# A fused attention and MoE kernel: a written-out order that interleaves one batch's attention with the preceding batch's MoE, heads in pairs on TensorE, attention output made transposed

## The chip, the core and the metric

One core of one Trainium2 chip runs the whole program. The metric is device time in microseconds (us), the median of several executions. The engines are named as in the profile: PE (TensorE; PEld are its weight loads), DVE (VectorE), ACT (ScalarE), POOL (GpSimd) and SP (SyncE, which here only issues transfers). Each works through its own queue in order; an instruction that waits holds up what is behind it on that engine.

## The reference

Two stages with sizes B = 8 batches, H = 12 heads, S = 448 positions, D = 64, and for the MoE 3584 tokens, 768 model columns and 2048 hidden columns; everything is float32 outside.

```python
def _attn_ref(q, k, v, g_q, g_k):
    def rmsnorm(x, g):
        rms = np.sqrt(np.mean(x * x, axis=-1, keepdims=True) + 1e-06)
        return x / rms * g
    q_n, k_n = (rmsnorm(q, g_q), rmsnorm(k, g_k))
    scores = np.matmul(q_n, k_n.transpose(0, 1, 3, 2)) / np.sqrt(q.shape[-1])
    ...
    return softmax(scores) @ v

def _moe_ref(x, w_in, w_out, alpha):      # x: heads side by side, one row per token
    h = x @ w_in
    s = np.sin(alpha * h)
    g = h + s * s / (alpha + 1e-09)
    return g @ w_out
```

The quotation writes the softmax in one line; "snake" below means the step from h to g.

## The kernel before

It is written with a tile framework whose scheduler orders the instructions of each engine by itself and places every wait. There are two stages, one after the other.

**Attention** (L70 to L151) runs over 8 batches and, in each, over 6 pairs of heads. q, k and v of a whole batch come by one transfer each (L80 to L82; 112 positions on the partitions, four blocks of them), v on POOL's queue because it is cast to bf16. Per head DVE squares and sums q and k (L92, L93), ACT takes the root (L95), DVE the reciprocal (L97) and, for each block of 112 positions, scales and multiplies by the gain (L99). PE transposes a pair's blocks (L109, L112), and DVE copies each from PSUM (L110, L113). Then, for each head, four score matmuls contract over that head's 64 partitions (L125), and ACT's Exp writes the weights with keys on the partitions (L129). The product with V (L133) holds a 112 by 112 piece of the weights stationary and streams V's 64 columns with a column of ones beside them (L120, L121): 16 matmuls of 65 columns per head, so that the output has positions on the partitions and the softmax sum in column 65. DVE divides (L140, L141), and because the MoE wants model columns on the partitions, PE transposes the result again (L147) and DVE copies it into `xT` (L148). All eight batches of `xT` stay in SBUF.

**MoE** (L160 to L213) holds both weight matrices in SBUF; their transfers (L169, L170) are issued on POOL's queue once the attention stage's SBUF is free. Over 8 groups of 448 tokens: for each of 16 blocks of 128 hidden columns, six matmuls (L183) make `hps`, ACT takes Sin (L190), DVE squares (L192) and adds (L193) into `g_sb`. Then, for each of four blocks of 112 tokens and two halves of 384 columns, 16 matmuls (L201), a copy (L208) and a store of 168 KB (L209).

Of the kernel before, what the change touches and what calls it, by code (L numbers as in the profile page):

```python
# [25 lines left out]
ALU = mybir.AluOpType  # L26


@with_exitstack
def kernel(  # L30
# [11 lines left out]
):  # L42
    nc = tc.nc
    B, H, S, D = q.shape
    N_TOK = B * S
    D_MODEL = H * D
    D_FF = moe_w_in.shape[1]
    KT = D_MODEL // 128
    MT = D_FF // 128
    P = 128  # L50

    SCORE_SCALE = float(D) ** 0.5

    SQB = 4
    SKB = 4
    sq_sz = S // SQB
    sk_sz = S // SKB

    const = ctx.enter_context(tc.tile_pool(name="const", bufs=1))
    gq_sb = const.tile([P, 1, D], F32)  # L60
# [4 lines left out]
    make_identity(nc, ident)  # L65

    xpool = ctx.enter_context(tc.tile_pool(name="xT", bufs=1))
    xT_b = [xpool.tile([P, KT, S], BF16, tag=f"xT{bb}", name=f"xT{bb}") for bb in range(B)]

    with tc.tile_pool(name="attn_in", bufs=2) as ain, \  # L70
         tc.tile_pool(name="attn_w", bufs=3) as awork, \
         tc.tile_pool(name="attn_wT", bufs=2) as awT, \
         tc.tile_pool(name="attn_sc", bufs=3, space=bass.MemoryType.PSUM) as scps, \
         tc.tile_pool(name="attn_tp", bufs=2, space=bass.MemoryType.PSUM) as tpps, \
         tc.tile_pool(name="attn_av", bufs=3, space=bass.MemoryType.PSUM) as avps:
        for b in range(B):
            qall = ain.tile([sq_sz, H, SQB, D], F32, tag="qall")
            kall = ain.tile([sq_sz, H, SQB, D], F32, tag="kall")
            vall = ain.tile([sq_sz, H, SQB, D], BF16, tag="vall")
            nc.sync.dma_start(out=qall, in_=q[b].rearrange("h (t p) d -> p h t d", p=sq_sz))  # L80
            nc.sync.dma_start(out=kall, in_=k[b].rearrange("h (t p) d -> p h t d", p=sq_sz))
            nc.gpsimd.dma_start(out=vall, in_=v[b].rearrange("h (t p) d -> p h t d", p=sq_sz))  # L82
            for hp in range(H // 2):
                h0 = 2 * hp
                qn = awork.tile([sq_sz, SQB, 2 * D], BF16, tag="qn")
                kn = awork.tile([sq_sz, SQB, 2 * D], BF16, tag="kn")
                for hi in range(2):
                    h = h0 + hi
                    for (xin, xout, gs) in ((qall[:, h], qn, gq_sb), (kall[:, h], kn, gk_sb)):
# [154 lines left out]
```

## Time and profile before

| what | value |
|---|---|
| median of three runs (lowest, highest) | 1063.31 us (1063.0, 1063.66) |
| span of the profiled execution | 1061.3 us |
| mean granted TensorE clock over the span | 0.995 |
| one transfer of q, k: size, median from issue to landing | 1344 KB, 8.6 us and 18.8 us |
| one transfer of v: size as stored, median from issue to landing | 672 KB, 15.1 us |
| bytes read from HBM, written | 45.69 MB, 11.01 MB |

The profile is of one execution. A busy time is the time in which an engine had at least one instruction running, so a group's busy time divided by its count can be less than its mean duration: matmuls overlap in PE's pipeline. "Idle before" is how long an engine stood still just ahead of a group's instructions, with an arrow to what ended that. The chain of waits goes back from the last instruction to what released each step. The granted clock is TensorE's, as a share of full speed. In tables of stretches times are counted from the span's start.

### The profile page before, as it was taken

How to read it: one execution, taken by the hardware profiler on the slowest of the kernel's cores; microseconds unless marked ns; L12 is line 12 of the kernel's file. 1: busy time of each engine (PE TensorE's matmuls, PEld its weight loads, DVE VectorE, ACT ScalarE, POOL GpSimd, SP SyncE). 2: the span in 40 equal slices, each digit the busy share in tenths (PEclk: the TensorE clock that was granted, in tenths of full speed). 3: DMA queues.
4: the chain of work that ended last, by engine and by line, in shares of the span. 5: the costliest groups of instructions: out<-in, count | busy, mean ns of one | idle time of the engine just before them, and what ended most of it. 6: DMA issues, size and time to landing. Idle time of an engine off the chain costs nothing.

```text
span 1061.3 us, 13360 instructions
## 1 busy us (share of the span) xinstructions
PE 813.0 (77%) x4288; PEld 486.0 (46%) x4288; DVE 697.4 (66%) x3201; ACT 422.4 (40%) x801; POOL 18.7 (2%) x16
## 2 busy tenths in 40 slices
PE   0677777777777777777777777737999999999998
PEld 0334444444444444444443444413656656656665
DVE  0777777777777777777777777613575665665754
ACT  0444445555445544555544554412131231221221
POOL 1000000000000000000000000000000000000000
PEclk9999999999999999999999999998999999999999
DMA  9701800900900900810540000075101101101001
GB/s 148 114 1 31 101 0 1 131 1 1 130 1 1 130 1 1 99 33 1 74 57 1 1 0 1 1 130 108 46 7 53 41 14 53 33 20 53 23 31 53
DMA packets 142870, 45.75 MB, mean 43 GB/s; under 512 B 132816, under 2 KB 142032, under 8 KB 142800
## 3 DMA queue, kind: packets, MB, share of 16 engines
q1 hardware_dynamic: 96816, 33.11, 15.9%
q0 software_dynamic: 45984, 11.80, 11.1%
q8 instruction: 33, 0.54, 0.2%
q14 instruction: 37, 0.30, 0.1%
HBM read 45.69 MB, written 11.01 MB: 53 GB/s over the span
## 4 chain that ended last, share of the span: by engine, by line
PE 60%; DVE 22%; ACT 9%; DMA 6%; issue 2%; SPq 0%; POOL 0%; ACTq 0%
PE av L133 17%; PE ops L201 16%; PE hps L183 13%; PE sc L125 12%; DVE kn L99 7%; ACT L129 6%; DVE qn L99 4%; DMA w_out_sb<-in_moe_w_out_dram 3%; DMA kall<-in_k_dram 2%; ACT expT L129 2%; DVE xT L148 2%; DVE invs L140 2%; DVE qT L110 2%; DVE ssq L93 2%; PE tp L109 1%
## 5 line engine op out<-in xcount | busy, mean ns | idle before, releaser
L133 PEld LDWEIGHTS <-expT 112*112 112x112 bf16 x1536 | 164.3, 204 | 147.6 <-DVE outn L141 56.7
L129 ACT ACTIVATE expT<-sc 112x448 bf16<-112x448 f32 x384 | 187.8, 544 | 73.2 <-PE sc L125 72.7
L133 PE MATMUL av<-vA,expT 112*112 112x65 bf16 x1536 | 202.2, 286 | 18.4 <-DVE outn L141 18.3
L125 PE MATMUL sc<-qT,kT 64*112 64x448 bf16 x384 | 193.6, 580 | 18.5 <-ACT expT L129 9.3
L183 PE MATMUL hps<-xT,w_in_sb 128*128 128x448 bf16 x768 | 169.4, 360 | 26.4 <-DMA w_in_sb<-in_moe_w_in_dram 17.5
L201 PE MATMUL ops<-w_out_sb,g_sb 128*112 128x384 bf16 x1024 | 185.6, 327 | 5.2 <-DMA w_out_sb<-in_moe_w_out_dram 5.2
L190 ACT ACTIVATE s<-hps,alpha_sb 128x448 f32<-128x448 f32 x128 | 81.1, 634 | 242.5 <-PE hps L183 207.9
L109 PE MATMUL tp<-ident,qn 112*128 112x112 bf16 x192 | 49.6, 258 | 140.1 <-DVE qn L99 101.8
L140 DVE RECIPROCAL invs<-av 112x1 f32<-112x1 f32 x384 | 50.3, 168 | 160.5 <-PE av L133 160.2
L201 PEld LDWEIGHTS <-g_sb 128*112 128x112 bf16 x1024 | 132.0, 130 | 49.5 <-issue 5.7
L95 ACT ACTIVATE rms<-ssq 112x4 f32<-112x4 f32 x192 | 29.1, 197 | 279.6 <-DVE ssq L93 273.2
L192 DVE TENSOR_TENSOR s<-s 128x448 f32<-128x448 f32 x128 | 79.8, 624 | 80.2 <-ACT s L190 80.2
L183 PEld LDWEIGHTS <-w_in_sb 128*128 128x128 bf16 x768 | 75.8, 99 | 101.6 <-issue 44.8
L193 DVE SCALAR_TENSOR_TENSOR g_sb<-s,inv_alpha_sb,hps 128x448 bf16<-128x448 f32 x128 | 87.0, 680 | 4.5
L208 DVE COPY osb<-ops 112x384 f32<-112x384 f32 x64 | 34.2, 555 | 74.7 <-PE ops L201 63.4
L99 DVE SCALAR_TENSOR_TENSOR qn<-qall,inv_rms,gq_sb 112x64 bf16<-112x64 f32 x384 | 83.3, 278 | 0.0
L99 DVE SCALAR_TENSOR_TENSOR kn<-kall,inv_rms,gk_sb 112x64 bf16<-112x64 f32 x384 | 83.0, 278 | 0.0
L125 PEld LDWEIGHTS <-kT 64*112 64x112 bf16 x384 | 64.3, 182 | 39.3 <-issue 25.6
L93 DVE TENSOR_REDUCE ssq<-sqv 112x4 f32<-112x256 f32 x192 | 74.5, 408 | 0.1
L109 PEld LDWEIGHTS <-qn 112*128 112x128 bf16 x192 | 20.6, 107 | 117.2 <-DVE qn L99 114.4
L112 PE MATMUL tp<-ident,kn 112*128 112x112 bf16 x192 | 49.3, 257 | 25.3 <-DVE kn L99 24.6
L141 DVE TENSOR_TENSOR outn<-av,invs 112x64 bf16<-112x64 f32 x384 | 65.5, 212 | 0.2
(24 smaller groups left out, 481.3 us busy)
## 6 DMA issues: line engine op xcount, KB each, us to landing
qall<-in_q_dram SPq DMA_DIRECT2D x8, 1344.0 KB, 8.6
kall<-in_k_dram SPq DMA_DIRECT2D x8, 1344.0 KB, 18.8
out_dram<-osb SPq DMA_DIRECT2D x64, 168.0 KB, 2.1
vall<-in_v_dram POOLq DMA_DIRECT2D x8, 672.0 KB, 15.1
w_in_sb<-in_moe_w_in_dram POOLq DMA_DIRECT2D x1, 3072.0 KB, 17.9
w_out_sb<-in_moe_w_out_dram POOLq DMA_DIRECT2D x1, 3072.0 KB, 32.7
gq_sb<-in_g_q_dram SPq DMA_DIRECT2D x1, 32.0 KB, 3.2
gk_sb<-in_g_k_dram SPq DMA_DIRECT2D x1, 32.0 KB, 4.4
```

The source lines that it names most:

```text
L93: nc.vector.reduce_sum(ssq, sqv, axis=AX.X)
L99: nc.vector.scalar_tensor_tensor(xout[:, t, hi * D:(hi + 1) * D], xin[:, t, :], inv_rms[:, t:t + 1], gs[:sq_sz, 0, :], op0=ALU.mult, op1=A ...
L109: nc.tensor.transpose(tp, qn[:, t, :], ident[:sq_sz, :sq_sz])
L125: nc.tensor.matmul(sc[:, :S], kT[pbase:pbase + D, t * sk_sz:(t + 1) * sk_sz], qT[pbase:pbase + D, :], start=True, stop=True,)
L129: nc.scalar.activation(expT[:, t, :], sc[:, :S], ACT.Exp, scale=SCORE_SCALE)
L133: nc.tensor.matmul(av, expT[:, t, u * sq_sz:(u + 1) * sq_sz], vA[:, t, :], start=(t == 0), stop=(t == SKB - 1),)
L140: nc.vector.reciprocal(invs, av[:, D:D + 1])
L183: nc.tensor.matmul(hps, w_in_sb[:, kt, m * P:(m + 1) * P], xT[:, kt, :], start=(kt == 0), stop=(kt == KT - 1),)
L190: nc.scalar.activation(s1, hps, ACT.Sin, scale=alpha_sb[:, m, :])
L192: nc.vector.tensor_mul(s2, s1, s1)
L193: nc.vector.scalar_tensor_tensor(g_sb[:, m, :], s2, inv_alpha_sb[:, m, :], hps, op0=ALU.mult, op1=ALU.add,)
L201: nc.tensor.matmul(ops, g_sb[:, m, ts * TOK_SUB:(ts + 1) * TOK_SUB], w_out_sb[:, m, dm * DM_TILE:(dm + 1) * DM_TILE], start=(m == 0), stop ...
```

## The change

The kernel's body is rewritten, and the framework's own ordering is switched off: every engine executes in the order in which the program writes its instructions. The framework still places waits, and gives out the four PSUM slots of two banks each (`bank_pair`) that all matmul outputs now share.

- **Loads.** q, k and v come by half batch ("group": 6 heads, 3 pairs). The 448 positions are three blocks of 128 and a rest of 64; the rests of two heads share one slot of 128 partitions, so that a group is 21 slots. Each load is five transfers; q and k go on SP's queue, v on POOL's. The first group is asked for before anything else, the weights after the first norm (`w_in`) and after batch 0's first pair (`w_out`).
- **Norm.** One group's norm is 24 small tasks over 7 slots (448 columns) at a time: squares on POOL, sums on DVE, the inverse root as a power of -0.5 on POOL, both gains multiplied into k on POOL, scaling on DVE. `bg(n)` takes the next n of them from a list at fixed places in the order. ACT has no Sqrt any more.
- **Pairs of heads.** Score matmuls alternate between partitions 0 to 63 (one head) and 64 to 127 (the other), into the two banks of a slot; one Exp covers both, 896 columns.
- **Transposed output.** `attend` holds V (64 columns of one head) stationary and streams the Exp tile's 448 columns; the heads' outputs lie on partitions 0 to 63 and 64 to 127, which is `xT`'s layout. The same stream with 64 columns of ones gives the softmax sum on every partition. ACT makes its reciprocal as Exp(-Ln(x)) from a table set that holds both functions; DVE multiplies into `xT`. The transposes of L147 and their copies go.
- **Order.** While batch b's six pairs run, the second product of batch b-1 is dealt out in steps of two matmuls between them (`fill`). Batch b's first product follows alone, its first four blocks begun without the last pair. Batch 0 has nothing to fill with, and the last batch's second product runs by itself at the end.
- **Tokens.** The second product takes 128 tokens at a time; the 64 left over of an even and an odd batch are put side by side, so that an odd batch has four such steps and an even one three. A store has 768 columns.
- **Snake.** The square is on POOL for even blocks and on ACT for odd ones instead of DVE.

What follows is the added code, without the removed body (it is the one printed above) and without tile declarations, weight loads and helpers of a line or two. SLOTS is 21, CH 7, NT 3, REST 64, GH 6, GP 3, NP 6, KT 6, MT 16.

```diff
+    ctx.enter_context(tc.manual_schedule())
...
+    wpool = ctx.enter_context(tc.tile_pool(name="weights", bufs=1))
+    inp = ctx.enter_context(tc.tile_pool(name="inp", bufs=3))
+    vpool = ctx.enter_context(tc.tile_pool(name="vpool", bufs=4))
+    sqpool = ctx.enter_context(tc.tile_pool(name="sq", bufs=3))
+    xpool = ctx.enter_context(tc.tile_pool(name="xT", bufs=2))
+    gpool = ctx.enter_context(tc.tile_pool(name="g", bufs=1))
+    psum = ctx.enter_context(tc.tile_pool(name="ps", bufs=4, space=bass.MemoryType.PSUM))
...
+    def load_group(src, dst, gi, eng):
+        b, h0 = gi // 2, (gi % 2) * GH
+        for t in range(NT):
+            eng.dma_start(
+                out=dst[:, t * GH:(t + 1) * GH, :],
+                in_=src[b, h0:h0 + GH, t * P:(t + 1) * P, :].rearrange("h p d -> p h d"),
+            )
+        rest = src[b, h0:h0 + GH, NT * P:S, :].rearrange("(pr two) p d -> two p pr d", two=2)
+        for hi in range(2):
+            eng.dma_start(out=dst[hi * 64:(hi + 1) * 64, NT * GH:SLOTS, :], in_=rest[hi])
...
+    load_v(0)
+    load_qk(1)
...
+        def square(which, c):
+            src = (qf, kf)[which][gi]
+            st[which, c] = sqpool.tile([P, CH, D], F32, tag="sq", name="sq")
+            nc.gpsimd.tensor_mul(st[which, c], src[:, c * CH:(c + 1) * CH, :], src[:, c * CH:(c + 1) * CH, :])
+        def reduce(which, c):
+            nc.vector.reduce_sum(st["ms"][:, which, c * CH:(c + 1) * CH], st[which, c], axis=AX.X)
+        def fold_g(c):
+            sl = kf[gi][:, c * CH:(c + 1) * CH, :]
+            nc.gpsimd.tensor_mul(sl, sl, gg.to_broadcast([P, CH, D]))
...
+        def rsqrt():
+            st["inv"] = npool.tile([P, 2 * SLOTS], F32, tag="inv", name="inv")
+            nc.gpsimd.tensor_tensor(
+                st["inv"], st["ms"].rearrange("p a s -> p (a s)"), mhalf.to_broadcast([P, 2 * SLOTS]), op=ALU.pow)
+        def scale(which, c):
+            src, dst = (qf, kf)[which][gi], (qn, kn)[which][gi]
+            lo = which * SLOTS + c * CH
+            nc.vector.tensor_mul(
+                dst[:, c * CH:(c + 1) * CH, :], src[:, c * CH:(c + 1) * CH, :],
+                st["inv"][:, lo:lo + CH].unsqueeze(2).to_broadcast([P, CH, D]))
...
+        work = [begin]
+        pend = None
+        for which in range(2):
+            for c in range(NCH):
+                work.append(lambda w=which, c=c: square(w, c))
+                if pend:
+                    work.append(pend)
+                pend = lambda w=which, c=c: reduce(w, c)
+        work.append(lambda: fold_g(0))
+        work += [pend, mean, rsqrt, lambda: fold_g(1), lambda: fold_g(2)]
+        for which in range(2):
+            for c in range(NCH):
+                work.append(lambda w=which, c=c: scale(w, c))
+        return work
...
+    def transposes(pi):
+        gi, pl = pi // GP, pi % GP
+        tp = psum.tile([P, 2, 1024], BF16, tag="ps", name="tp")
+        for which, src in ((0, qn[gi]), (1, kn[gi])):
+            o = tp[:, 0, which * S:(which + 1) * S]
+            m0, r0 = token_columns(pi // NP)
+            for t in range(NT):
+                nc.tensor.transpose(o[:, m0 + t * P:m0 + (t + 1) * P], src[:, t * GH + 2 * pl:t * GH + 2 * pl + 2, :], ident)
+            for hi in range(2):
+                r = slice(hi * 64, hi * 64 + 64)
+                nc.tensor.transpose(o[r, r0:r0 + REST], src[r, NT * GH + pl, :], ident[r, r])
+        qkT[pi] = tpool.tile([P, 2, S], BF16, tag="qkT", name="qkT")
+        nc.vector.tensor_copy(qkT[pi], tp[:, 0, :2 * S].rearrange("p (a s) -> p a s", a=2))
+    def scores(pi, t):
+        sc = bank_pair("sc")
+        qt, kt = qkT[pi][:, 0, :], qkT[pi][:, 1, :]
+        m0, r0 = token_columns(pi // NP)
+        if t == 0:
+            expT[pi] = epool.tile([P, 2 * NT + 1, S], BF16, tag="expT", name="expT")
+        for hi in range(2):
+            r = slice(hi * 64, hi * 64 + 64)
+            if t < NT:
+                nc.tensor.matmul(sc[:, hi, :S], kt[r, m0 + t * P:m0 + (t + 1) * P], qt[r, :], start=True, stop=True)
+            else:
+                nc.tensor.matmul(sc[r, 0, :S], kt[r, r0:r0 + REST], qt[r, :], start=True, stop=True)
+        if t < NT:
+            nc.scalar.activation(expT[pi][:, 2 * t:2 * t + 2, :], sc[:, :, :S], ACT.Exp, scale=SCALE)
+        else:
+            nc.scalar.activation(expT[pi][:, 2 * NT, :], sc[:, 0, :S], ACT.Exp, scale=SCALE)
+    def attend(pi):
+        b, hp = pi // NP, pi % NP
+        gi, pl = pi // GP, pi % GP
+        e = expT[pi]
+        av = bank_pair("av")
+        for bank in range(2):
+            for t in range(NT + 1):
                 for hi in range(2):
+                    r = slice(hi * 64, hi * 64 + 64)
+                    if t < NT:
+                        lhsT = vb[gi][:, t * GH + 2 * pl + hi, :] if bank == 0 else ones
+                        rhs = e[:, 2 * t + hi, :]
+                    else:
+                        lhsT = vb[gi][r, NT * GH + pl, :] if bank == 0 else ones[r, :]
+                        rhs = e[r, 2 * NT, :]
+                    nc.tensor.matmul(av[r, bank, :S], lhsT, rhs, start=(t == 0), stop=(t == NT))
+        rec = rpool.tile([P, S], F32, tag="rec", name="rec")
+        nc.scalar.activation(rec, av[:, 1, :S], ACT.Ln)
+        nc.scalar.activation(rec, rec, ACT.Exp, scale=-1.0)
+        if hp == 0:
+            xT[b] = xpool.tile([P, KT, S], BF16, tag="xT", name="xT")
+        nc.vector.tensor_mul(xT[b][:, hp, :], av[:, 0, :S], rec)
...
+    def snake(b, hps, m):
+        s1 = spool.tile([P, S], F32, tag="s1", name="s1")
+        nc.scalar.activation(s1, hps, ACT.Sin, scale=alpha_sb[:, m, :])
+        s2 = spool.tile([P, S], F32, tag="s2", name="s2")
+        if m % 2 == 0:
+            nc.gpsimd.tensor_mul(s2, s1, s1)
+        else:
+            nc.scalar.activation(s2, s1, ACT.Square)
+        def finish():
+            nc.vector.scalar_tensor_tensor(
+                g_sb[:, m, (b % 2) * S:(b % 2 + 1) * S], s2, inv_alpha_sb[:, m, :], hps, op0=ALU.mult, op1=ALU.add)
+        return finish
+    def first_product(b):
+        x = xT[b]
+        late = deque()
+        def mm(ps, m, kts):
+            for kt in kts:
+                nc.tensor.matmul(ps[:, m % 2, :S], w_in_sb[:, kt, m * P:(m + 1) * P], x[:, kt, :],
+                                 start=(kt == 0), stop=(kt == KT - 1))
+        EARLY = 4
+        tiles = {}
+        for m in range(EARLY):
+            if m % 2 == 0:
+                tiles[m // 2] = bank_pair("hps")
+            mm(tiles[m // 2], m, range(KT - 1))
+        for m in range(MT):
+            if m < EARLY:
+                mm(tiles[m // 2], m, [KT - 1])
+            else:
+                if m % 2 == 0:
+                    tiles[m // 2] = bank_pair("hps")
+                mm(tiles[m // 2], m, range(KT))
+            late.append(snake(b, tiles[m // 2][:, m % 2, :S], m))
+            if len(late) > 1:
+                late.popleft()()
+            bg(1)
+        while late:
+            late.popleft()()
+    def second_product(b):
+        steps = []
+        for i in range(NT + b % 2):
+            st = {}
+            def step(m, i=i, st=st):
+                if m == 0:
+                    st["ps"] = bank_pair("ops")
+                c0 = (b % 2) * S + token_columns(b)[0] + i * P if i < NT else NT * P
+                lhsT = g_sb[:, m, c0:c0 + P]
+                for half in range(2):
+                    nc.tensor.matmul(st["ps"][:, half, :HALF], lhsT, w_out_sb[:, m, half * HALF:(half + 1) * HALF],
+                                     start=(m == 0), stop=(m == MT - 1))
+                if m == MT - 1:
+                    osb = opool.tile([P, 2, HALF], F32, tag="osb", name="osb")
+                    nc.vector.tensor_copy(osb, st["ps"][:, :, :HALF])
+                    o = osb.rearrange("p a d -> p (a d)")
+                    if i < NT:
+                        r0 = b * S + i * P
+                        nc.sync.dma_start(out=out[r0:r0 + P, :], in_=o)
+                    else:
+                        for hi in range(2):
+                            r0 = (b - 1 + hi) * S + NT * P
+                            nc.sync.dma_start(out=out[r0:r0 + REST, :], in_=o[hi * 64:hi * 64 + REST, :])
+            steps += [lambda m=m, s=step: s(m) for m in range(MT)]
+        return steps
...
+    background.extend(norm_tasks(0))
+    bg(len(background))
+    load_v(1)
+    load_weights()
+    transposes(0)
+    transposes(1)
+    background.extend(norm_tasks(1))
+    for b in range(B):
+        nc.scalar.preload_act_table_set(EXP_LN)
+        if b:
+            fillers.extend(second_product(b - 1))
+        n_fill = len(fillers)
+        if b + 1 < B:
+            load_qk(2 * b + 2)
+            load_v(2 * b + 2)
+        for p in range(NP):
+            pi = b * NP + p
+            quota = (n_fill * (p + 1)) // NP - (n_fill * p) // NP
+            part = [quota * j // 4 for j in range(5)]
+            scores(pi, 0)
+            scores(pi, 1)
+            bg(2)
+            if p:
+                attend(pi - 1)
+            fill(part[1])
+            bg(2)
+            scores(pi, 2)
+            fill(part[2] - part[1])
+            bg(2)
+            scores(pi, 3)
+            fill(part[3] - part[2])
+            if b == 0 and p == 0:
+                bg(len(background))
+            if pi + 2 < B * NP:
+                transposes(pi + 2)
+            fill(part[4] - part[3])
+            bg(2)
+            if b + 1 < B:
+                if b == 0 and p == 0:
+                    load_w_out()
+                if p == 0:
+                    background.extend(norm_tasks(2 * b + 2))
+                if p == 2:
+                    bg(len(background))
+                    load_qk(2 * b + 3)
+                    load_v(2 * b + 3)
+                    background.extend(norm_tasks(2 * b + 3))
+        fill(len(fillers))
+        attend(b * NP + NP - 1)
+        first_product(b)
+        bg(len(background))
+    for s in second_product(B - 1):
+        s()
```

216 lines of the change are left out of this document (69 added, 147 removed).

## The prediction

> **What bounds the kernel now.** I read the page's busy shares and its chain of waits first, then the table by stretches, then the chain in order of time for one stretch of each stage, last the groups of instructions for durations. The busy shares (busy us, share of the span, instructions) and the chain:
>
> ```profile
> span 1061.3 us, 13360 instructions
> PE 813.0 (77%) x4288; PEld 486.0 (46%) x4288; DVE 697.4 (66%) x3201; ACT 422.4 (40%) x801; POOL 18.7 (2%) x16
> PE 60%; DVE 22%; ACT 9%; DMA 6%; issue 2%; SPq 0%; POOL 0%; ACTq 0%
> ```
>
> No engine is full, and the chain hops between three: a handover problem, but not everywhere. Stretches (start:end, length, busy us of PE, PEld, DVE, ACT, POOL, granted clock, DMA share, GB/s):
>
> ```profile
> 0.00:40.00 40.00, 6.63 (x28) 3.36 (x28) 13.25 (x62) 6.53 (x13) 4.77 (x8) 1.00 1.35 164
> 642.49:656.41 13.92, 10.12 (x52) 5.79 (x52) 10.38 (x62) 7.08 (x14) 0.00 (x0) 1.00 0.00 0
> 690.00:720.00 30.00, 11.79 (x55) 6.15 (x54) 3.11 (x21) 5.61 (x10) 1.99 (x2) 1.00 0.77 140
> 720.00:740.00 20.00, 12.74 (x46) 6.08 (x46) 8.10 (x13) 3.90 (x7) 0.00 (x0) 0.74 0.58 106
> 950.00:1000.00 50.00, 49.04 (x272) 30.81 (x271) 31.87 (x51) 13.32 (x21) 0.00 (x0) 1.00 0.09 28
> ```
>
> Until about 698 us attention runs alone, after 731 us the MoE; between them PE waits for weights. The MoE keeps PE busy 49 of 50 us, attention 10.1 of 13.9 us, with few columns moved in that time. The second row is one head pair, cut from one L147 transpose to the next in the chain (start, length, what):
>
> ```profile
> 642.49 0.27 PE tpo L147
> 656.41 0.27 PE tpo L147
> 678.21 0.55 PE sc L125
> 680.14 0.92 PE sc L125 x2
> 681.07 1.65 PE av L133 x14
> 698.66 32.68 DMA w_out_sb<-in_moe_w_out_dram
> 732.50 4.16 PE hps L183 x12
> 746.83 0.97 PE ops L201 x6
> 747.81 2.42 PE hps L183 x12
> 1042.47 14.99 PE ops L201 x91
> ```
>
> 48 pairs of 13.92 us are 668 of the 1061 us. In the MoE an L183 matmul (448 columns) goes at 2.42/12 = 0.202 us and an L201 one (384) at 0.97/6 = 0.162, in a long run 14.99/91 = 0.165. In attention a second score matmul, also 448 columns, adds 0.92 - 0.55 = 0.37 us, nearly twice 0.202. The same factor shows where the MoE begins: 4.16/12 = 0.35 us, in the stretch with the granted clock at 0.74. So I read attention as running at half the array clock although its rows say 1.00; half the array's rows being in use is the other reading, and the two come apart below.
>
> **The change, part by part.** Durations (out<-in, count | busy, mean ns | idle before):
>
> ```profile
> L129 ACT ACTIVATE expT<-sc 112x448 bf16<-112x448 f32 x384 | 187.8, 544 | 73.2 <-PE sc L125 72.7
> L193 DVE SCALAR_TENSOR_TENSOR g_sb<-s,inv_alpha_sb,hps 128x448 bf16<-128x448 f32 x128 | 87.0, 680 | 4.5
> L190 ACT ACTIVATE s<-hps,alpha_sb 128x448 f32<-128x448 f32 x128 | 81.1, 634 | 242.5 <-PE hps L183 207.9 <-DVE s L192 34.6
> L192 DVE TENSOR_TENSOR s<-s 128x448 f32<-128x448 f32 x128 | 79.8, 624 | 80.2 <-ACT s L190 80.2
> L183 PEld LDWEIGHTS <-w_in_sb 128*128 128x128 bf16 x768 | 75.8, 99 | 101.6 <-issue 44.8
> L93 DVE TENSOR_REDUCE ssq<-sqv 112x4 f32<-112x256 f32 x192 | 74.5, 408 | 0.1
> L129 ACT ACT_TABLE_LOAD x48 | 61.6, 1283 | 0.9
> L95 ACT ACTIVATE rms<-ssq 112x4 f32<-112x4 f32 x192 | 29.1, 197 | 279.6 <-DVE ssq L93 273.2 <-DVE kT L113 5.7
> L92 DVE TENSOR_TENSOR sqv<-qall 112x256 f32<-112x256 f32 x96 | 39.8, 415 | 0.0
> L208 DVE COPY osb<-ops 112x384 f32<-112x384 f32 x64 | 34.2, 555 | 74.7 <-PE ops L201 63.4
> L82 POOL DMA_DIRECT2D vall<-in_v_dram x8 | 16.1, 2007 | 506.0 <-DVE qT L110 423.9 <-DVE kT L113 81.7 <-issue 0.4
> masks.py:199 POOL TENSOR_SCALAR_AFFINE_SELECT ident<-ident 128x128 bf16<-128x128 bf16 x1 | 0.3, 306 | 0.1
> ```
>
> *PE, one pair.* The 32 `av` matmuls of 65 columns, paced by 1.65/14 = 0.118 us, become 16 of 448 columns with V (or ones) stationary and the output already transposed; the four L147 transposes go. Scores stay 8 matmuls of 448 columns. Each two neighbours now use disjoint halves of the array. No row shows two matmuls sharing the array, so the bounds are 0.202 us for two (full overlap) and 0.404 (none). I take full overlap: the two share neither rows and banks (scores) nor columns and output partitions (`av`), and weight loads hide behind a stream (99 ns beside 0.202). Scores 4 x 0.202 = 0.81; `av` 8 x 0.202 = 1.62; transposes ten, at a weight load of 0.10 each, 1.0. The second product brings (4 x 48 + 4 x 64) x 2 = 896 matmuls instead of 1024, or 18.7 per pair: 18.7 x 0.162 = 3.0. Changing the array's shape costs something: a lone score between `av` runs takes 0.55 against 0.37 for a further one, so 0.18, and at full clock half, 0.09; about eleven changes per pair are 1.0 us (bounds 0 and 2). Sum 7.4 us a pair, 44.6 for six.
>
> The Trainium skill ("TensorEngine Tiling (Array Packing)", Tiling Modes, Key Properties) speaks against such a mix: changing the tiling mode drains TensorE. The 0.18 us agrees, though scores on 64 partitions beside `av` on 112 are the only change of shape the trace has. Of the overlap the same skill ("TensorE: Matmul & The Clock Gate", Part 3) measures 2.38 times from three column tiles; if two kept that share (0.79) of the ideal, my estimate would rise by about 0.65 us a pair, 31 us in all.
>
> *PE, first product.* 96 x 0.202 = 19.4 us per batch, nothing else between but the last `attend`. Its latency (Ln, Exp, multiply, about 2 us by the rows above) is covered by 20 early matmuls, 4.0 us; without them it would cost 8 x 2 = 16 us.
>
> *What must hide.* ACT, one pair: an Exp in series takes 187.8/384 = 0.49, and from 197 ns for 4 columns to 544 for 448 each column takes 0.78 ns, so 896 columns take 0.84; three of these and three short ones (the last Exp tile, Ln, Exp) are 4.0 us, under 7.4. Two table loads per batch (2.6 us) instead of 96 in all. In the first product ACT has 16 x 0.634 + 8 x 0.54 = 14.5 us, under 19.4. DVE, one fused batch: 24 norm steps of 448 columns x 0.62 = 14.9, six copies of 896 (0.624 + 448 x 1.1 ns = 1.1 us, the slope from 415 to 624 ns over 192 columns) and six multiplies of 0.65: 10.5, output copies 3.5 x 0.97 = 3.4; 29 us under 44.6. GpSimd: 18 norm multiplies and 8 for the snake per batch; the trace has no such multiply; the nearest row, 306 ns for 128 columns, gives 1.07 us, 27.8 in all; lower bound 0.62 (DVE's own), upper open. Ten V loads at about 0.75 (half a V is half of 2.0 us, cut into five) add 7.5; two power steps, in no row, I take as 3 us each (bounds 0.2, 50). 41 us per batch, under 64.
>
> *Waits added.* DVE works in the order written. Its reductions and scalings wait for GpSimd's squares and power and, behind two `load` calls, for q and k; queued behind them are the multiply that frees `av`, the copy of the next transposes, and the output copies that free `ops`, for all of which PE waits once its four PSUM pairs are held. Worst is the end of the third pair, where the remaining tasks are emptied, so that the fourth pair's DVE work stands behind a power (3) and six scalings (3.7), against some 4 us of slack: 3 to 5 us per batch; I take 4 (bounds 0, 12). SP's output stores stand before later loads; at 4 stores a batch that is nothing.
>
> *Start.* No fillers in batch 0. Input rows come at 164 GB/s: 1.38 MB of q and k for half a batch in 8.4 us, with V and the fixed part about 12. GpSimd and DVE finish the norm by about 22, first scores at 24. Pairs 0 and 1 at 5 us (7.4 - 3.0, some at half clock): 34. The copy for pair 2 is queued behind the whole norm of the second group: 10. Four pairs 20, half clock and late data 5, the last `attend` and first product 23: 92 us. The transfers agree: 8.3 MB of inputs at 164 GB/s (50 us) and two weights of 18 us, by
>
> ```profile
> out_dram<-osb SPq DMA_DIRECT2D x64, 168.0 KB, 2.1
> w_in_sb<-in_moe_w_in_dram POOLq DMA_DIRECT2D x1, 3072.0 KB, 17.9
> ```
>
> are 86 us. Bounds 75 and 115.
>
> *Sum.* Start 92; seven batches of 44.6 + 19.4 + 4 = 68: 476; last second product 128 x 0.162 = 20.7; copy 1.0 and store 2.1. Span 592. The profiled execution spans 1061.3 us and the median of the runs is 1063.3; with the same 2 us around it, **594 us**.
>
> **The rivals.** *No overlap* (A): PE does two halves one after the other: 48 x 12 x 0.202 = 116 us more, 710. For: no row shows overlap; against: disjoint halves throughout.
>
> *Half clock stays* (B): array time in the fused part doubles as in attention now: a pair 14.8, a batch 89 + 19.4 + 4 = 112, seven 787, start about 120: 930; 1,070 with the first product slow as well (7 x 19.4). For: attention at 0.37 us per matmul. Against: PE there moves few columns, while fused it streams nearly without gaps, as from 740 us, where 0.202 holds.
>
> *Queues behind GpSimd* (C): multiplies at about 2 us and the in-order DVE cost 12 to 16 us per batch, not 4: 97 + 7 x (76 to 80) + 26 = 655 to 683. For: the squares are on the path of every scaling. Against: 41 us of work in 64.
>
> *GpSimd becomes the bound* (D), slower: every batch then takes GpSimd's time. It decides above 64 us a batch, and passes 1063 when a batch takes (1063 - 92 - 26)/7 = 135 us: multiplies at (135 - 13.5)/26 = 4.7 us, or power steps of 50 us. Say 6 us a multiply: 170 a batch, 1,310 us. For: the trace prices neither operation. Against: 306 ns for 128 columns, a quarter of that rate. The Trainium skill ("GPSIMD Engine Reference", Performance versus the Vector engine) has 4497 ns for 2048 columns, by which a multiply here would be an estimated 1 us; no row here shows one.
>
> That the interleaving isn't in the code is excluded: PE's order is written out.
>
> **How the numbers follow.** Forecast 0.57, its own range 530 to 650 (start 17 less or 23 more, changes of shape 48 either way, waits 28 less or more, though hardly all at one end). A 0.17, C 0.14, B 0.07, D 0.05. 530 to 730 holds the forecast's case, A and C but for their tails, leaving about 0.2 out. Faster 0.94, within 0.2% 0.01, slower 0.05 (D, and B's worst end); 0.2% is about what a measurement here can tell, the three runs lying within 0.06%.
>
> **What would show it.** Two neighbouring `sc` or `av` matmuls starting within some 20 ns and ending 0.2 us later: overlap; starts 0.2 us apart: A; 0.37: B. First product batches of 19 to 21 us. GpSimd's square near 1.07 us, power near 3. PE over 90% busy in fused batches, its longest idle time in the fourth pair, ended by DVE; a reduction or scaling that waits for GpSimd for 10 us or more: C. First scores near 24 us, first second-product matmul near 92. The forecast is wrong if a batch from the second on takes under 58 or over 80 us.

## The result, and the profile after

| kernel | median (lowest, highest), us | ratio to before [95%] | profiled span, us | clock |
|---|---|---|---|---|
| before, four runs beside those of after | 1063.15 | 1 | 1061.3 | 0.995 |
| after, four runs | 744.19 (739.98, 750.16) | 0.7004 [0.6968, 0.704] | 739.9 | 0.908 |

The change takes 30% off the time: faster, as forecast, but 150 us more than 594. That is 94 us past the forecast's own range of 530 to 650, and 14 us past the 530 to 730 that was to hold rivals A and C as well. The page after, with the same three views as the page before (span, busy shares, chain):

```profile
span 739.9 us, 8666 instructions
PE 542.2 (73%) x3296; PEld 237.9 (32%) x3296; DVE 322.8 (44%) x464; ACT 333.8 (45%) x496; POOL 385.9 (52%) x312
PE 40%; ACT 15%; POOL 15%; DVE 14%; issue 8%; SPq 5%; DMA 2%; DVEq 0%; ACTq 0%; POOLq 0%
```

PE has 271 us less to do, but it is busy 73% of the span where it was 77%, and it carries a smaller part of the chain than before: 40% against 60%; the rest goes from engine to engine. GpSimd, 2% busy before, is the second busiest engine. (The execution profiled for experiment 8 below, 593.17 us, is a slow one: it is left out of that experiment's time, and its rows are used for the order of events alone.)

The table by stretches says where. The rows below are cut at the first matmuls of the stages: batch 0's attention; the fused part of batch 2 and its first product; the fused part of batch 7. The columns are start:end, length, busy us of PE, PEld, DVE, ACT, POOL, granted clock, DMA share, GB/s.

```profile
32.87:93.96 61.09, 32.28 (x206) 11.95 (x204) 32.88 (x44) 23.50 (x34) 54.70 (x40) 0.75 1.02 159
212.10:271.20 59.10, 48.39 (x333) 21.26 (x332) 27.35 (x37) 26.49 (x37) 40.08 (x30) 0.91 0.37 56
271.20:298.40 27.20, 19.75 (x100) 9.29 (x100) 13.15 (x22) 15.16 (x25) 7.70 (x9) 1.00 0.29 66
646.10:686.90 40.80, 39.55 (x282) 16.55 (x282) 9.76 (x14) 26.48 (x37) 0.00 (x0) 1.00 0.05 21
```

Batch 7 has no further batch to norm, and its fused part has no hole: 39.55 of 40.80 us are PE's. In batch 2 PE stands still for 10.7 us of the fused part, and for 7.5 of the 27.2 of the first product. Added up over the batches and set beside the terms of the forecast:

| stage | forecast, us | measured, us | difference |
|---|---|---|---|
| to the end of batch 0's first product | 92 | 128.1 | +36 |
| seven fused parts, waits included | 340 | 382 | +42 |
| seven first products | 136 | 203 | +67 |
| last second product, copy, store | 24 | 26 | +2 |

The groups of instructions and the waits name two suspects (waits: us in total, times, longest; groups: as in the prediction's fence):

```profile
L289 PE MATMUL hps<-xT,w_in_sb 128*128 128x448 bf16 x768 | 171.7, 373 | 65.9 <-ACT s L270 56.2 <-DVE xT L264 6.5 <-DVE qkT L223 3.2
L172 POOL TENSOR_TENSOR inv<-ms,mhalf 128x42 f32<-128x42 f32 x16 | 113.4, 7087 | 63.2 <-DVE ms L168 62.9
L178 DVE TENSOR_TENSOR qn<-qf,inv 128x448 bf16<-128x448 f32 x48 | 57.6, 1251 | 85.1 <-POOL inv L172 85.1
L178 DVE TENSOR_TENSOR kn<-kf,inv 128x448 bf16<-128x448 f32 x48 | 47.8, 1035 | 0.0
L158 POOL TENSOR_TENSOR sq<-kf 128x448 f32<-128x448 f32 x48 | 43.7, 928 | 52.5 <-DVE ms L161 52.5
```

```profile
DVE qn L178 <- POOL inv L172: 85.1, 16, 7.2
PE hps L289 <- ACT s L270: 56.2, 64, 1.7
```

**First suspect: the power.** One GpSimd power of 42 columns takes 7.09 us, 169 ns a column, where a GpSimd multiply of 448 columns takes 0.93. Behind it a scaling takes 1.25 us (q) and 1.04 us (k) on average, where 0.62 was put. The timeline around the fourth pair of batch 3 (start, length, engine, what, idle time before) shows them in series, and PE at the end of it:

```profile
325.56 3.55 DVE L178 TENSOR_TENSOR qn<-qf,inv 128x448 bf16<-128x448 f32 x3 [7.20 <-POOL inv L172]
329.03 4.28 DVE L178 TENSOR_TENSOR kn<-kf,inv 128x448 bf16<-128x448 f32 x3
333.24 0.61 DVE L264 TENSOR_TENSOR xT<-av,rec 128x448 bf16<-128x448 f32 x1
...
318.44 7.09 POOL L172 TENSOR_TENSOR inv<-ms,mhalf 128x42 f32<-128x42 f32 x1 [3.29 <-DVE ms L168]
...
333.90 0.48 PE L218 MATMUL tp<-ident,qn 128*128 128x128 bf16 x3 [10.20 <-DVE xT L264]
```

PE's row blames the multiply into `xT` (L264), a 0.61 us instruction; it is late because it stands behind 7.2 us of waiting and 7.8 us of scaling on an in-order engine.

**Second suspect: a wait on Sin.** The first product's matmuls wait 64 times, 8 in each batch, for ACT's Sin. From the timeline of batch 1's first product:

```profile
201.23 2.43 PE L289 MATMUL hps<-xT,w_in_sb 128*128 128x448 bf16 x12 [0.78 <-ACT s L270]
204.44 0.35 PE L289 MATMUL hps<-xT,w_in_sb 128*128 128x448 bf16 x1 [0.78 <-ACT s L270]
...
202.62 0.63 ACT L270 ACTIVATE s<-hps,alpha_sb 128x448 f32<-128x448 f32 x1 [1.44 <-PE hps L289]
203.28 0.58 ACT L275 ACTIVATE s<-s 128x448 f32<-128x448 f32 x1
203.77 0.62 ACT L270 ACTIVATE s<-hps,alpha_sb 128x448 f32<-128x448 f32 x1
```

Twelve matmuls, two blocks of six, run without a pause, then PE stands until Sin has finished: the next begin 3.21 us after the first, where 12 x 0.19 would be 2.3 (the last PE row is cut off by the end of the stretch asked for). Two hidden blocks lie in the two banks of one slot of `bank_pair`. The code runs block m's six matmuls, its Sin, then block m+1's six into the other bank of that slot. So the wait could be for a tile that ACT is still reading, though in its other bank; or for ACT and the snake being too slow to give slots back at all.

**What was right is in the trace as well.** A pair in the clean part of batch 2:

```profile
218.64 0.55 PE L234 MATMUL sc<-qkT 64*128 64x448 bf16 x4
219.13 1.06 PE L258 MATMUL av<-expT,vb 128*64 128x448 bf16 x8
220.12 1.06 PE L258 MATMUL av<-expT,ones 128*64 128x448 bf16 x8
```

Four score matmuls of 448 columns in 0.55 us: the second two add 0.19 us together. Taken singly, the two of a step start 3 ns apart and the next two 0.2 us later, which is the sign of overlap that the prediction named. The eight `av` matmuls on `ones` start 0.99 us after the eight on `vb`, in four steps of two: 4 x 0.19 = 0.76, and 0.23 more. Most of the 0.23 lies around the step with the rest of 64 keys: it starts 0.29 us after the step ahead of it, and the step behind it 0.31 us later.

### The profile page after: what moved, and what is told of

It reads as the page before. It is cut to its first block, busy times and chain, and to the rows that moved or that the text cites. A ratio compares the mean times of both kernels' runs of the same rounds, so it can differ in the third digit from the quotient of the medians.

```text
span 739.9 us, 8666 instructions
## 1 busy us (share of the span) xinstructions
PE 542.2 (73%) x3296; PEld 237.9 (32%) x3296; DVE 322.8 (44%) x464; ACT 333.8 (45%) x496; POOL 385.9 (52%) x312
## 4 chain that ended last, share of the span: by engine, by line
PE 40%; ACT 15%; POOL 15%; DVE 14%; issue 8%; SPq 5%; DMA 2%; DVEq 0%; ACTq 0%; POOLq 0%
PE ops L324 13%; PE hps L289 13%; POOL inv L172 12%; ACT s L270 10%; PE av L258 7%; DVE kn L178 5%; ACT s L275 4%; DVE qn L178 4%; SPq L92 3%; PE sc L234 2%; POOL sq L158 2%; PE tp L218 2%; SPq L98 2%; DMA kf<-in_k_dram 1%; DVE qkT L223 1%
## 5 line engine op out<-in xcount | busy, mean ns | idle before, releaser
L238 ACT ACTIVATE expT<-sc 128x896 bf16<-128x896 f32 x144 | 125.7, 914 | 186.9 <-PE sc L234 186.8
L324 PE MATMUL ops<-w_out_sb,g_sb 128*128 128x384 bf16 x896 | 177.2, 331 | 0.0
L273 POOL TENSOR_TENSOR s<-s 128x448 f32<-128x448 f32 x64 | 59.6, 932 | 210.1 <-ACT s L270 188.2
L172 POOL TENSOR_TENSOR inv<-ms,mhalf 128x42 f32<-128x42 f32 x16 | 113.4, 7087 | 63.2 <-DVE ms L168 62.9
L324 PEld LDWEIGHTS <-g_sb 128*128 128x128 bf16 x896 | 74.5, 98 | 66.1 <-issue 28.3
L178 DVE TENSOR_TENSOR qn<-qf,inv 128x448 bf16<-128x448 f32 x48 | 57.6, 1251 | 85.1 <-POOL inv L172 85.1
L264 DVE TENSOR_TENSOR xT<-av,rec 128x448 bf16<-128x448 f32 x48 | 29.7, 619 | 105.1 <-ACT rec L261 105.1
L258 PE MATMUL av<-expT,vb 128*64 128x448 bf16 (+1 forms) x384 | 57.3, 399 | 3.8 <-ACT expT L238 3.3
L165 POOL TENSOR_TENSOR kf<-kf,gg 128x448 f32<-128x448 f32 x48 | 59.6, 1252 | 0.0
L161 DVE TENSOR_REDUCE ms<-sq 128x7 f32<-128x448 f32 x96 | 55.1, 609 | 6.9 <-POOL sq L158 6.8
L258 PE MATMUL av<-expT,ones 128*64 128x448 bf16 (+1 forms) x384 | 54.6, 384 | 0.0
```

The source lines that it names most:

```text
L165: nc.gpsimd.tensor_mul(sl, sl, gg.to_broadcast([P, CH, D]))
L172: nc.gpsimd.tensor_tensor(st["inv"], st["ms"].rearrange("p a s -> p (a s)"), mhalf.to_broadcast([P, 2 * SLOTS]), op=ALU.pow)
L178: nc.vector.tensor_mul(dst[:, c * CH:(c + 1) * CH, :], src[:, c * CH:(c + 1) * CH, :], st["inv"][:, lo:lo + CH].unsqueeze(2).to_broadcast( ...
L238: nc.scalar.activation(expT[pi][:, 2 * t:2 * t + 2, :], sc[:, :, :S], ACT.Exp, scale=SCALE)
L258: nc.tensor.matmul(av[r, bank, :S], lhsT, rhs, start=(t == 0), stop=(t == NT))
L273: nc.gpsimd.tensor_mul(s2, s1, s1)
```

## The experiments

**1. Both blocks before both Sins.** One edit in `first_product`: a slot's twelve matmuls are issued before its snakes.

```diff
 for m in range(MT):
-    if m < EARLY:
-        mm(tiles[m // 2], m, [KT - 1])
-    else:
-        if m % 2 == 0:
-            tiles[m // 2] = bank_pair("hps")
-        mm(tiles[m // 2], m, range(KT))
+    if m % 2 == 0:
+        if m >= EARLY:
+            tiles[m // 2] = bank_pair("hps")
+        for mi in (m, m + 1):
+            mm(tiles[m // 2], mi, [KT - 1] if m < EARLY else range(KT))
     late.append(snake(b, tiles[m // 2][:, m % 2, :S], m))
```

> Both blocks of a PSUM slot get their matmuls before either block's Sin is issued; nothing else moves. Theory W (the odd block's matmuls wait until ACT's Sin has read the even block in the other bank of the same slot): a clean first product falls from 27.2 us to about 20 (8 x 12 x 0.189, and 1.7 for the last pair), 7 to 8 us in each of eight batches, in all 670 to 695 us. Rival S (the snake's chain through ACT, GpSimd and DVE paces it, the slot coming free too late): less than 15 us saved, above 725.

Measured: 674.64 us (two runs, 673.34 and 675.95; ratio 0.6344 [0.6313, 0.6376]), 70 us less than after. A first product, and all that its matmuls still wait for, in the whole run:

```profile
253.80:272.50 18.70, 18.36 (x98) 9.27 (x96) 12.24 (x21) 14.21 (x24) 6.53 (x7) 1.00 0.44 96
```

```profile
PE hps L289 <- DVE xT L264: 6.3, 7, 4.1
PE hps L289 <- DVE qkT L223: 3.2, 3, 1.1
```

No wait on Sin is left, PE is busy 18.36 of 18.70 us, and ACT has its 14.2 us of work in the same stretch, so neither ACT nor the snake was too slow. The wait for the power is as long as in after, 84.9 us in all.

**2. Each block a slot of its own.** The same question from the other side: order as in after, but no two blocks share a slot (and three early blocks instead of four, so that the slots suffice).

```diff
-    nc.tensor.matmul(ps[:, m % 2, :S], w_in_sb[:, kt, m * P:(m + 1) * P], x[:, kt, :],
+    nc.tensor.matmul(ps[:, 0, :S], w_in_sb[:, kt, m * P:(m + 1) * P], x[:, kt, :],
...
-    if m % 2 == 0:
-        tiles[m // 2] = bank_pair("hps")
-    mm(tiles[m // 2], m, range(KT))
+    tiles[m] = bank_pair("hps")
+    mm(tiles[m], m, range(KT))
```

> First product in the order of the changed kernel, but each block of 128 hidden columns has a PSUM slot of its own (three early blocks instead of four); the power stays on GpSimd. If PE waits because two blocks share a slot: a clean first product is 19 to 21 us, as with the other order of matmuls, in all 670 to 695 us. Rival (PE waits for the snake itself because the order gives ACT each block late): 25 us or more, above 725.

Measured: 679.54 us (two runs, 679.43 and 679.65; 0.6389 [0.6371, 0.6408]); first products of 19.3 to 23.1 us from batch 1 on. What the matmuls wait for:

```profile
PE hps L289 <- DVE qkT L223: 12.8, 7, 4.6
PE hps L289 <- DVE g_sb L278: 6.6, 7, 1.0
PE hps L289 <- DVE xT L264: 2.1, 5, 0.4
```

Again no Sin. With the order kept, the sharing alone made the wait: a write to one bank of a slot was held until the read of the other bank was done. The trace shows it as a wait that ACT's instruction ends; the matmuls that run keep their pace. What is left, 21.5 us in the three rows, ends with DVE's instructions; after had 9.7 us of such waits.

**3. The power on ACT.** The inverse root becomes Exp(-0.5 Ln(x)), from the table set that attention uses; the set is also asked for ahead of the first norm, so that its load is not on the path of the start.

```diff
-    nc.gpsimd.tensor_tensor(
-        st["inv"], st["ms"].rearrange("p a s -> p (a s)"), mhalf.to_broadcast([P, 2 * SLOTS]), op=ALU.pow)
+    nc.scalar.activation(st["inv"], st["ms"].rearrange("p a s -> p (a s)"), ACT.Ln)
+    nc.scalar.activation(st["inv"], st["inv"], ACT.Exp, scale=-0.5)
```

> The inverse root is Exp(-0.5 Ln(x)) on ACT, two instructions of 42 columns, instead of GpSimd's power of 7.09 us; ACT's table set holds both already. Theory Q (DVE's queue stands behind the power, and PE behind DVE): PE's idle time of 9 to 10 us in the fourth pair falls to 2 to 4, first scores come at about 26 us instead of 32.9, batch 0 loses some 20 us in all, the odd batches' first product some 3; in all 655 to 690 us. Rival L (late q and k, or scalings slowed by GpSimd, hold DVE): the idle time falls by less than 2 us, above 725.

Measured: 648.47 us (648.17 to 648.77; 0.6098 [0.6081, 0.6116]), 96 us less than after and less than any of the expected times. A first product, a fused part, and the waits in question:

```profile
231.60:258.30 26.70, 19.58 (x98) 9.26 (x96) 9.70 (x16) 15.18 (x25) 7.67 (x9) 1.00 0.30 67
258.30:303.30 45.00, 41.27 (x301) 17.62 (x300) 26.82 (x42) 27.23 (x41) 25.55 (x28) 1.00 0.44 64
```

```profile
DVE qn L179 <- ACT inv L174: 5.2, 9, 0.6
PE hps L290 <- ACT s L271: 56.8, 64, 1.7
```

PE's hole of 9 to 10 us shrinks to 2.5 in half of the batches and is gone in the others. The seven fused parts sum to 320 us instead of 382, the first 112 us replace 128, and the first products sum to 188 instead of 203: the norm's late remainder had run into them too. The expectation had some 3 us for that in the odd batches; what it missed is mostly in the fused parts, which fall by 62 us, where six holes going from 9 or 10 us to between 2 and 4 would be 30 to 48. A part of the rest is PE's pace: the second to the sixth fused part of after read a clock of 0.88 to 0.91, the same parts here 1.00, and PE's busy time in one of them falls by about 2 us. The wait on Sin is the same to 1%, so the two suspects are separate.

**4. Both edits.**

> The order of the matmuls in the first product and the inverse root on ACT together. If the two causes are separate idle times of PE, the savings add: 744 - 70 - 96 = 578, range 570 to 592 us; first product 18 to 19 us from the second batch on, fused part 41 to 48. Rival: part of both savings is the same idle time (late scalings push the first product's additions), 595 to 615 us.

Measured: 589.94 us (four runs, 586.36 to 592.88; 0.5543 [0.5515, 0.5571]), clock 0.953. It is 154 us less than after, where the two edits alone save 70 and 96: nearly additive. The page, and then batch 0's attention, the fused part of batch 3 and its first product:

```profile
span 588.3 us, 8601 instructions
PE 516.4 (88%) x3296; PEld 234.8 (40%) x3296; DVE 293.9 (50%) x464; ACT 336.0 (57%) x529; POOL 266.0 (45%) x296
```

```profile
24.96:83.60 58.64, 36.59 (x206) 13.01 (x204) 36.57 (x51) 24.28 (x40) 36.39 (x39) 0.67 1.16 182
237.10:284.20 47.10, 42.83 (x302) 17.81 (x302) 27.70 (x44) 27.75 (x42) 26.68 (x29) 0.96 0.42 62
284.20:302.40 18.20, 18.20 (x98) 9.27 (x96) 8.79 (x15) 14.22 (x24) 6.53 (x7) 1.00 0.48 97
```

Without these two waits the stages stand near the prediction's terms: 331 us of fused parts (340 forecast), 128 of first products (136), 103 for the start (92).

**5. Heads one after the other.** In after, `av` for all blocks of one head and then of the other, so that neighbours share columns and partitions. Rival A made by hand, for `av` only.

```diff
-    for t in range(NT + 1):
-        for hi in range(2):
+    for hi in range(2):
+        for t in range(NT + 1):
```

> In the product with V all four matmuls of one head go ahead of the other head's, so that neighbours use the same half of the array; same work, same result. If the overlap is worth what its starts show (two matmuls in 0.19 us): 48 x 8 x 0.19 = 73 us more, a pair 8.3 us instead of 6.8, in all 800 to 820 us. Rival (the pair is set by ACT or by waits, PE has room): less than 25 us more.

Measured: 811.01 us (810.35 to 811.66; 0.7627 [0.7605, 0.7649]), 67 us more than after. The same instructions in a clean pair of batch 1:

```profile
143.24 0.55 PE L234 MATMUL sc<-qkT 64*128 64x448 bf16 x4
143.72 2.05 PE L258 MATMUL av<-expT,vb 128*64 128x448 bf16 x8
145.69 1.06 PE L258 MATMUL av<-expT,ones 128*64 128x448 bf16 x4
```

Eight matmuls now start 1.97 us ahead of what follows, where it was 0.99. The pairs with nothing waiting grow by 1.96 us (two such groups of eight), and the fourth pair of a batch by nothing, since its hole of 10 us has room for it. So the order of two loops is worth 67 us here, through the overlap.

**6. No interleaving**, in after and in the version of experiment 4: the second product of the preceding batch runs as one block ahead of the six pairs.

```diff
+    fill(len(fillers))
     for p in range(NP):
```

> The second product of the preceding batch runs as one block ahead of the batch's attention instead of between its pairs. Theory: a pair alone is bound by ACT's 4.0 us and its handovers, about 4.7, against 3.8 of PE; a clean batch's fused part 41 to 44 becomes 18 + 28 = 46, and the idle time of the fourth pair grows by 2 to 4 us as less covers it: 30 to 60 us more, 770 to 800 us. Rival 1 (PE, being idle for a sixth of the time, is granted half its clock as in the kernel before): a pair at 7 us or more, over 840 us. Rival 2 (PE bound either way): less than 10 us more.

> The run with both, and the preceding batch's second product as one block ahead of the attention. What interleaving is worth once the long waits are gone: if a pair alone takes 4.6 to 5.0 us (ACT's 4.0 and handovers) against 3.8 of PE, a batch is 3 to 6 us longer, in all 610 to 635 us. Rival 1 (DVE's norm work no longer fits in the shorter attention and stalls it): above 645. Rival 2 (PE bound either way): within 8 us of 590.

Measured: 789.73 us (789.37 to 790.09; 0.7427 [0.7405, 0.7448]), 46 us more than after; and 627.62 us (626.27 to 628.97; 0.5901 [0.587, 0.5932]), 38 more than experiment 4. From after without interleaving, six pairs by themselves and PE's wait:

```profile
329.70:372.50 42.80, 28.21 (x206) 11.45 (x205) 21.04 (x31) 23.07 (x34) 30.71 (x20) 0.76 0.50 82
```

```profile
PE av L258 <- DVE xT L264: 73.3, 13, 11.7
```

A pair alone, clear of the norm's wait, takes 4.55 to 5.05 us. That is the surprising size: of the 13.92 us that a pair took before, most is saved without any second product between the pairs, by the new form of attention and by PE's full pace (before's attention ran at half of it, see the next section). Of the 474 us that experiment 4 saves against before, 436 are there without interleaving. What interleaving adds is 38 to 46 us in all: it fills holes, and the clock is higher with it too (0.908 against 0.872, 0.953 against 0.918); no run separates the two.

**7. What slows the scalings?** In after, a scaling takes 0.61 us alone, one of q 1.25 on average behind the power, and GpSimd multiplies the gains into k at that moment. On the version of experiment 4, that multiplication goes ahead of the inverse root.

```diff
-    work.append(lambda: fold_g(0))
-    work += [pend, mean, rsqrt, lambda: fold_g(1), lambda: fold_g(2)]
+    work += [lambda: fold_g(0), lambda: fold_g(1), lambda: fold_g(2)]
+    work += [pend, mean, rsqrt]
```

> As the run with both, and GpSimd multiplies the gains into k for all three chunks before the inverse root instead of beside the scalings. Contention theory (a DVE multiply with two SBUF inputs takes 1.55 us beside a GpSimd multiply and 0.61 alone): the fourth pair of odd batches falls from 9.5 to about 7.5 us, in all 10 to 18 us less than with both. Rival (squares and the V loads behind them slow the scalings as much, and the sums come later): less than 5 us.

Measured: 591.06 us (584.87 to 592.02; 0.5544 [0.5514, 0.5573]), no difference from 589.94. The scalings of q, in experiment 4 and here:

```profile
L179 DVE TENSOR_TENSOR qn<-qf,inv 128x448 bf16<-128x448 f32 x48 | 35.6, 794 | 5.2 <-ACT inv L174 5.2
```

```profile
L179 DVE TENSOR_TENSOR qn<-qf,inv 128x448 bf16<-128x448 f32 x48 | 37.1, 826 | 5.2 <-ACT inv L174 5.2
```

They got no shorter, and those of k hardly (33.4 us busy before the edit, 30.5 with it), so the expected gain is not there. The traces say why: the premise came from after, where 32 of the 96 scalings run beside the gains' multiplication. In experiment 4, with the power gone, only 2 of the 96 still do, and 69 have no GpSimd instruction beside them and take 0.61 to 0.63 us. Most of the slow ones that are left stand beside squares and V loads, at up to 1.69 us, and this edit leaves those where they are. In detail, the fourth pair of batches 1, 3 and 5 falls from between 9.5 and 10.2 us to 8.4, and that of 2, 4 and 6 grows from 7.5 to 7.8.

**8. The start.** On top of 7, batch 0's queue on GpSimd is reordered: the V load of group 1 goes ahead of the first norm and that of group 2 behind the second, the product of the two gains (which waits for a small transfer) out of the way of DVE's first sums.

```diff
-    nc.vector.tensor_mul(gg, gq_sb, gk_sb)
...
+    if gi == 0 and c == 0:
+        nc.vector.tensor_mul(gg, gq_sb, gk_sb)
...
+    load_v(1)
     bg(len(background))
-    load_v(1)
...
-    load_v(2 * b + 2)
+    if b:
+        load_v(2 * b + 2)
...
     bg(len(background))
+    load_v(2)
```

> As the run before it, and batch 0's queue on GpSimd is ordered anew: the V load of group 1 ahead of the first norm, that of group 2 behind the second norm, and the gains' product only where it is first used, so that DVE's first sums don't wait for it. Theory (GpSimd's descriptor work and the wait for the gains stand ahead of the squares): first scores 2 to 4 us earlier, the 12 us idle before the third pair falls to 4 to 8, in all 6 to 12 us less. Rival (the second group's rows arrive no earlier, or the weights come later): less than 3 us, or slower.

Measured: 586.32 us (three runs, 583.9 to 586.79; 0.5505 [0.5492, 0.5519]); this interval overlaps those of experiments 4 and 7, so the gain is not established. In the profiled execution first scores come at 26.7 us, against 25.0 in experiment 4, so nothing shows an earlier start. In its first 90 us GpSimd's squares wait for the transfers of k, as they do in experiment 4 (10.3 us there):

```profile
POOL sq L158 <- DMA kf<-in_k_dram: 17.8, 4, 10.0
```

The theory that GpSimd's queue holds the start is not confirmed.

## Why the prediction was off, point by point

**The direction, the overlap and the terms of a pair held.** Full overlap: 0.19 us for two matmuls of 448 columns (0.202 put), and 67 us lost when it is taken from `av` alone. Rival A is out. The Trainium skill ("TensorE: Matmul & The Clock Gate", Part 3), whose 2.38 from three column tiles I had turned into an estimate of 31 us more, does not carry over: two halves give all of a factor of two here. A change of shape: 0.09 put, about 0.11 measured. The Trainium skill ("TensorEngine Tiling (Array Packing)", Key Properties) has a change of tiling mode drain TensorE; a small cost at the changes agrees, and it is cheap here. A clean pair: 7.4 put; 6.84 in batches with 16 filling matmuls per pair and 7.81 in those with 21, a mean of 7.26. GpSimd's multiply: 1.07 put, 0.93 to 1.04 measured for squares, a median of 1.13 for the gains' multiplication into k. Tail: 24 put, 26 measured.

**The half clock.** The prediction left two readings of 0.37 us per score matmul open. The same instruction, on 64 partitions in both cases, decides it. Two rows of after's timeline, and the stretches around them (the clock is the third column from the end):

```profile
32.88 1.30 PE L234 MATMUL sc<-qkT 64*128 64x448 bf16 x6
...
59.95 0.93 PE L234 MATMUL sc<-qkT 64*128 64x448 bf16 x4 [0.28 <-DVE qkT L223]
```

```profile
32.90:37.00 4.10, 4.10 (x26) 1.52 (x26) 0.62 (x1) 3.50 (x5) 3.67 (x6) 1.00 1.54 203
59.00:64.00 5.00, 4.31 (x22) 1.25 (x22) 4.06 (x8) 1.73 (x2) 2.98 (x4) 0.50 1.16 202
```

Four of them take 0.93 us where the row gives the clock as 0.50, and 0.55 us in the clean pair at 218.64, in a stretch that reads 1.00. So 64 partitions are not slow in themselves. At 32.88 six take 1.30, the 0.37 per two of the half clock, while the row reads 1.00. The reason lies in the column: the trace of after has no clock record ahead of 37.6 us, that of before none ahead of 719 us, and the column reads 1.00 where there is none. Just behind before's first record its L183 matmuls go at 0.19 us where the record says 1.00 and at 0.37 where it says 0.50. So before's 0.37 in attention is half pace, as the prediction read it, and the 0.995 stated for before's whole span says nothing about its first 719 us. Rival B, that the half clock stays in the fused part, did not come: the fused part of batch 7, which has no hole, reads 1.00, that of batch 2, with its hole, 0.91.

**Step that failed first, the first product: "96 x 0.202 = 19.4 us per batch, nothing else between but the last `attend`."** It took 26.6 to 31.3 us from batch 1 on. I checked that ACT's 14.5 us fit beneath and never asked in which order PE and ACT touch a slot: two blocks in one slot, with a Sin between their matmuls, make PE wait for ACT eight times a batch. Experiments 1 and 2 take the wait away in two ways and give 18.2 to 20.1 us and 19.3 to 23.1; alone this is 65 to 70 of the 150 us. None of my rivals had it. The row "0.202 us per matmul" was a price for the matmul, not for the loop.

**Step that failed second: "two power steps, in no row, I take as 3 us each", and "six scalings (3.7)".** They took 7.09 and 7.8: 15 us in series where I had 6.7, against the same slack, so a wait of 9 to 10 us per batch instead of 4. The place was right (the fourth pair, ended by DVE) and so was the mechanism, an in-order DVE behind GpSimd; this is rival C's mechanism, though with a dearer power, not with multiplies of 2 us. The value 3 came from no row, between bounds of 0.2 and 50, and the range should have paid for that. The cost was larger than the hole: the delayed norm also ran into the first products (203 us against 188 without the power) and the start, and PE's clock read lower in the fused parts with the hole. Taking the power away gave 96 us.

**The start** came at 128 instead of 92: 16 of the 36 us by the power (four of them in batch 0's path), 9 by the wait on Sin (112 in experiment 3 against 103 in experiment 4), and 11 remain there. First scores were put at 24 us; they come at 32.9 in after and at 25.0 in experiment 4. What holds batch 0's pairs after that is not settled. Squares that wait for k's transfers and a slow PE are in the trace: the clock reads 0.67 over batch 0's pairs in experiment 4, where PE is busy 36.59 us with 206 matmuls, against 28.21 us for 206 in the six pairs of experiment 6.

**GpSimd as the bound** (rival D) did not come: 385.9 of 739.9 us busy.

With both failed steps mended on the chip, the kernel takes 589.94 us, where 594 was forecast. Part of that nearness is errors that offset each other (start +11, fused parts and first products -17); but it says that those two steps, and no third of their size, made the difference.

Experiment 4 stands at 0.5543 of before's time, 154 us under after; the later edits (0.5544 and 0.5505) are not shown to better it.

## What to carry to other kernels

When an order is written by hand, check for every pair of engines that share a buffer in which order they touch it, not only whether the work of one fits beneath the other's: half a slot was enough for 0.9 us, 64 times. An operation that no row prices, on a chain that an in-order engine waits for, belongs in the range at its dear end, and first on the list to be measured. When a rewrite moves several things at once, price the wait that each leaves next; here two waits, each cheap to remove, held a third of the gain. And before you trust a clock column that reads 1.00, see whether the matmuls go at the pace of full clock: here it read 1.00 all through before's attention, which ran at half pace.

## What was not expected of the hardware

- A GpSimd power costs 169 ns a column (7.09 us for 128 by 42), some 80 times its multiply (0.93 us for 448). One ACT activation of the same 42 columns takes 0.24 us in experiment 4, and the inverse root needs two:

```profile
L173 ACT ACTIVATE inv<-ms 128x42 f32<-128x42 f32 x16 | 3.8, 238 | 65.2 <-DVE ms L169 65.2
```

- DVE's scaling of 448 columns takes 0.61 us in each of the 28 cases in after that have no GpSimd instruction beside them, and 1.54 to 1.56 in the 32 beside the gains' multiplication. The tile view of after, for q (minimum, median, maximum in ns):

```profile
L178 DVE TENSOR_TENSOR qn<-qf,inv x48: 610/1545/1556, 26.2 to 616.4; 128x448 bf16<-128x448 f32 x48
```

  The long time exceeds the short one by 0.93 us, where the gains' multiplication itself takes 1.12 at the least. The Trainium skill ("SBUF — State Buffer", Who interferes with whom) has a rule for such a pair: a DVE operation with two inputs in SBUF and a GpSimd one that reads SBUF exclude each other, and the loser waits for the whole instruction. That fits roughly, if the multiplication starts a little ahead. But 25 scalings with only a V load's issue beside them take up to 1.40 us too (median 1.35), and no run took GpSimd away, so the cause stays argued.
- A copy of 896 bf16 columns from PSUM on DVE takes 0.62 us, where 1.1 was put from the slope of float32 operations with two inputs; DVE had more room than the sum gave it.
